# Linear attention and a feed-forward block in one kernel: products of four tiles at a time, loads of the attention units issued by ScalarE, two more denominators computed early

## The chip, the cores and the metric

The kernel runs on one NeuronCore of a Trainium2 chip, with TensorE (PE), VectorE (DVE), ScalarE (ACT), GpSimd (POOL) and SyncE (SP) as its engines. The metric is the device time of one execution in microseconds (us), as the median of several runs; lower is better. One of the executions was taken with a hardware profile, from which all views in this text come.

## The reference

A layer norm, multi-head linear attention with a learned feature map (two softmaxes over 32 values for each head, of a projection and of its negative), a residual; then a layer norm, a ReLU feed-forward block and a residual. There are 2048 tokens of width 1024, 32 heads of 32, and a hidden width of 3584, all in float32.

```python
qkv = layernorm(x) @ wqkv                    # (2048, 3 * 1024), 32 heads of 32
pq, pk = q @ w_phi[h], k @ w_phi[h]          # for each head
phi_q = concat(softmax(pq), softmax(-pq))    # 64 features a head; phi_k alike
kv = phi_k^T v ; z = sum over tokens of phi_k
o = (phi_q @ kv) / (phi_q @ z + 1e-6)
h = x + o @ wo
out = h + relu(layernorm(h) @ w1) @ w2
```

## The kernel before

**Products.** Every large product is made of three: TensorE multiplies a high and a low part of each operand (high x high, high x low, low x high; lines 181 to 183), 128x128 stationary and 128x512 moving. The parts of a weight tile come from `Units.advance`: ScalarE copies the loaded tile to the high part (line 124), and POOL or DVE subtracts to get the low part (line 128). Which of the two does it stands in `odd`. Tiles of w1 and w2 are also needed as sums and differences (the feed-forward block is multiplied by a seven-product scheme): `t_load` loads a set, `t_sum` makes four sums on POOL (line 378), `t_store` writes them to DRAM, from where they are loaded like weights later. There are 56 such sets.

**Order.** The work on TensorE is a list of items. An item is one 128-token tile against one group of weights: 8 steps, each of three multiplications (4 steps in the feed-forward part). Items 0 to 31 make keys and values of the first eight token tiles, in four slabs of 256 columns (eight items each); 32 to 47 the queries of these tiles; 48 to 79 keys and values of the last eight tiles; 80 to 95 their queries; 96 to 127 the output projection; then come the two products of the feed-forward block. Everything else is placed by hand at a step: `when(step, f, ...)` issues f behind step `step % 8` of item `step // 8`. What is issued goes to the engines' queues in that order, and each engine works through its own queue in order. SP issues nearly all DMAs, in order as well, and stands when one waits for a buffer.

**Keys and values.** Behind an item, `kv_first` (DVE) starts the softmax, `kv_exp` (ScalarE) and `kv_second` (DVE) finish it and leave `kphi` (line 472; four buffers), `kv_z` (POOL, line 480) adds it up, and `kv_third` (line 491) multiplies it with the values: 16 small multiplications a tile, 128x32 stationary. They are issued for three, three and two tiles of a slab together, at one place.

**Folds.** The projections' weights are multiplied with w_phi first, on TensorE: `fold_part(p)` (64 small multiplications, line 297; 32x32), `fold_turn` (DVE), `fold_store` to DRAM, and `fold_ready`, behind which the weights may be loaded. p = 0 to 3 are the four slabs, 4 to 7 the queries.

**Attention.** A unit u (32 of them) is four token tiles by 256 columns of features. `at_load` loads the exponentials of the queries (written to `ed` earlier), `at_sums` multiplies them with z on POOL (line 616, tile `ez`, one buffer), `at_reduce` sums on DVE (line 622), `at_den` (POOL, lines 631 and 635) and `at_inverse` (DVE) make the denominator, `at_scale` (POOL, lines 648 and 653) scales, `at_turn` (DVE, line 659) transposes 32x32 blocks, and `at_num` (TensorE, line 673) multiplies two units with kv; ScalarE copies the four results out, and `at_low` (DVE, line 690) makes the low parts. For units 0 to 5 (`EARLY`) load, sums, denominator and inverse are made once beside keys and values (`early_load` and so on), and the scale goes into a small tile; these units load again later and are only scaled. In each unit's list of steps, the denominators lie ahead of the unit's turn, and `at_num` follows some 30 steps behind the unit's start. Layer norm statistics of the second block (`ln_power` on POOL, `ln_pair`) lie between them.

**Opening.** Before item 0 and inside it, the first slab's weights are made: for each k of 8, `first_high` (ScalarE) copies a part of a PSUM tile, and `first_low` (DVE, line 415) subtracts from the same PSUM tile; two k share one.

Of the kernel before, what the change touches and what calls it, by code (L numbers as in the profile page):

```python
# [67 lines left out]
class Units:  # L68
# [35 lines left out]
    def advance(self, n):  # L104
# [7 lines left out]
        while self.done < self.loaded:  # L112
# [5 lines left out]
            if self.first[key] > n + SOON and n < max(self.asked[key] + LAG, self.latest + pace):  # L118
# [6 lines left out]
            odd = key[0] == "a" or key[0] in ("kv", "w1", "wo") and self.done % 2 or \  # L125
                key[:2] == ("q", 0) and key[-1] in (2, 5)
            eng = nc.vector if odd else nc.gpsimd
# [12 lines left out]
def kernel(  # L140
# [220 lines left out]
    def t_load(w, p, j, place):  # L361
        cols = slice(256 * j, 256 * (j + 1))
        if place is lnp:
            b = lnp.tile([P, D], F32, name="xin").rearrange("p (a f) -> p a f", a=4)
        else:
            b = place.tile([P, 4, 256], F32, name="b", bufs=2)
        src = (w1 if w == 1 else w2)[2 * p:2 * p + 2, :, :, cols]
        sp.dma_start(b, src.rearrange("a b p f -> p (a b) f"))
        for r in range(2):
            for c in range(2):  # L370
                tsum[j, r, c] = b[:, 2 * c + r if w == 1 else 2 * r + c, :]
        tsum[j] = b
# [210 lines left out]
    def at_load(u):  # L583

        e = lnp.tile([P, D], F32, name="xin") if u in (4, 5, 10, 11) else ap_.tile([P, D], F32, name="qe", bufs=4)
        e_q[u] = e = e.rearrange("p (h s f) -> p h s f", s=2, f=DH)
        sp.dma_start(e.rearrange("p (i c) s f -> p i (c s f)", i=4), ed[u // 8][:, u % 8])

    EARLY = 6

# [20 lines left out]
    def at_sums(u):  # L613
        b, q, r = UNITS[u]
        ez = ap_.tile([P, D], F32, name="ez", bufs=1).rearrange("p (i n) -> p i n", i=4)
        pool.tensor_tensor(out=ez, in0=e_q[u].rearrange("p (i h) s f -> p i (h s f)", i=4),  # L616
                           in1=zb[:, q, None, 256 * r:256 * (r + 1)].to_broadcast([P, 4, 256]), op=ALU.mult)
        ez_of[u] = ez

    def at_reduce(u):  # L620
        tz_of[u] = tz = ap_.tile([P, 32], F32, name="qtz", bufs=2)
        v.tensor_reduce(out=tz, in_=ez_of.pop(u).rearrange("p i (h f) -> p (i h) f", f=DH), op=ALU.add, axis=AX.X)

# [16 lines left out]
    def at_scale(u):  # L640
        if u < EARLY:
            e = e_q.pop(u).rearrange("p (i c) s f -> p i (c s) f", i=4)
# [331 lines left out]
    for i, j in enumerate((2, 3, 0, 1)):  # L974
# [3 lines left out]
        when(40, fold_ready, 0, j // 2)  # L978
    for p, n in zip(range(1, 8), (3, 8, 12, 16, 20, 24, 28)):
        do(n, 6 if p > 1 else 7, fold_part, p)  # L980
        if p > 1:
            when(8 * n + 10, fold_turn, p, (0, 1))
        for j in range(2):
            lag = 8 * n + 6 + 2 * j + (3 if p == 1 else 0)
            when(lag + (6 if p == 1 else 14), fold_store, p, j)
            when(lag + (13 if p == 1 else 24), fold_ready, p, j)
        do(max(n - 2, 1), 0, wt_load, p, sp)


    for (hf, s, t), n in kv_n.items():  # L990
        when(8 * n + 11, kv_exp, (hf, s, t))
        when(8 * n + 13, kv_second, (hf, s, t))
        when(8 * n + 18, kv_z, (hf, s, t))
        when(8 * (n + (2, 1, 0, 2, 1, 0, 1, 0)[t % HT]) + 22, kv_third, (hf, s, t))
        if hf == 1 and t == NT - 1:
# [67 lines left out]
    for u in range(32):  # L1063
        start = 8 * (a0 + u) if u >= 8 else 8 * (last_kv + 4) + 19 * u // 2
        slack = 6 if u < 5 else 0
        if u % 2:
            places = (-8 if u < 12 else -1, 6, 10, 13, 16, 19, 25)
            when(start + 30 + slack, at_num, u - 1)
            when(start + 32 + slack, at_low, u - 1)
        elif u < 16:  # L1070
            places = (-8 if u < 12 else -1, 6, 10, 13, 16, 19, 25)
        else:
            places = (6, 12, 16, 19, 21, 23, 29)
        for step, f in zip(places, (at_load, at_sums, at_reduce, at_den, at_inverse, at_scale, at_turn)):
            if u >= EARLY or f in (at_load, at_scale, at_turn):
                when(max(start + step, 8 * (last_kv + 4)), f, u)
        if u < EARLY:
            start = 8 * (kv_n[1, u // 2, NT - 1] + 3) + 4 + 18 * (u % 2)
            for step, f in ((0, early_load), (9, early_sums), (14, early_reduce), (16, at_den), (18, at_inverse),
# [50 lines left out]
    sets = [(w, p, j) for w in (1, 2) for p in range(NP) for j in range(2)]  # L1130
    places = [24 + 10 * n for n in range(22)] + [264, 274, 284, 294, 364, 374]
    slabs = [8 * kv_n[1, q, HT] for q in range(4)]
    places += sorted([slab + step for slab in slabs for step in (10, 24, 38)] + [slabs[1] + 2, slabs[2] + 2])
    places += [up0 + 440 + 25 * n for n in range(14)]
    for n, (step, (w, p, j)) in enumerate(zip(places, sets, strict=True)):
        far = n < 22
        when(step, t_load, w, p, j, lnp if step > up0 else fp if far and n % 4 > 1 else tsp)
        for k in range(4):
            when(step + (12 if far else 7) + k, t_sum, j, k)
        when(step + (19 if far else 13), t_store, w, p, j)  # L1140

# [72 lines left out]
    for k in range(2):  # L1214
        value_low(k, pool)
        first_high(k)
        first_low(k)
    first_fold(2)
# [3 lines left out]
    for k in range(2, 4):  # L1222
        first_high(k)
        first_low(k)
    ln_stats(("x", 1))
# [82 lines left out]
```

## Time and profile before

| | |
|---|---|
| time before, median of 3 runs | 1890.67 us (1890.42 to 1891.12) |
| the profiled execution | 1889.38 us, of which the span of instructions 1887.6 |
| busy: PE, DVE, ACT, POOL | 1876.9, 1070.4, 743.5, 983.7 us |
| granted TensorE clock | 1.000 |
| mean DMA rate | 229 GB/s |

In the views, a line of a timeline is start, length, engine, line of the code, operation, output <- inputs, shapes, and in brackets how long the engine stood before it and what ended that. "x" is a count. PEld is TensorE's weight load, which runs beside its multiplications. An engine that ends in q is the queue that issues.

### The profile page before, as it was taken

Reading aid. Unit: us, or ns where it says so; the run is one execution under the profiler, and the core shown is the slowest. Engines: PE = TensorE matmul, PEld = TensorE weight load, DVE = VectorE, ACT = ScalarE, POOL = GpSimd, SP = SyncE. Lnnn points to the kernel's source line nnn. Section 1 sums busy time; section 2 is a strip of 40 time slices with the busy share of each in tenths; the row PEclk is TensorE's granted clock in tenths of the full one; section 3 lists DMA queues with packets and bytes.
Section 4 is the critical chain, followed back from the end, with each engine's and each line's share of the span. In section 5 each row is a group of like instructions: output and inputs, shape, how many; then the busy total and the mean of one; then the engine's idle time right before and its main releaser. Section 6 shows DMA issues by size and latency. Waiting matters only on the chain.

```text
span 1887.6 us, 31801 instructions
## 1 busy us (share of the span) xinstructions
PE 1876.9 (99%) x11630; PEld 1538.0 (81%) x11630; DVE 1070.4 (57%) x1688; ACT 743.5 (39%) x1264; POOL 983.7 (52%) x934
## 2 busy tenths in 40 slices
PE   9999999999999999999999999999999999999999
PEld 7777888888888787888888888888888888888887
DVE  7888688676689667455444573445443433343333
ACT  5322244222233122354554554444344444444442
POOL 3888633677746888323333234544454444444443
PEclk9999999999999999999999999999999999999999
DMA  6799685454454666886777996787777677777775
GB/s 226 255 302 327 232 257 179 151 151 147 149 188 160 203 225 217 270 266 201 272 232 237 302 298 234 250 286 242 274 259 216 199 234 237 239 215 216 217 214 179
DMA packets 292749, 432.17 MB, mean 229 GB/s; under 512 B 24176, under 2 KB 150128, under 8 KB 292592
## 3 DMA queue, kind: packets, MB, share of 16 engines
q1 hardware_dynamic: 275424, 413.33, 68.3%
q10 hardware_dynamic: 17168, 16.81, 2.5%
q8 instruction: 91, 1.49, 0.3%
q14 instruction: 66, 0.54, 0.1%
HBM read 292.68 MB, written 137.36 MB: 228 GB/s over the span
## 4 chain that ended last, share of the span: by engine, by line
PE 92%; POOL 5%; DVE 2%; issue 1%; ACT 0%; DMA 0%; SPq 0%; POOLq 0%; DVEq 0%
PE mm L181 24%; PE mm L182 23%; PE mm L183 23%; PE ac L183 4%; PE ac L181 4%; PE ac L182 4%; PE tp L182 2%; PE tp L183 2%; PE tp L181 2%; POOL ez L616 1%; PE tp L250 1%; POOL qe L653 1%; PE ac L491 1%; PE tp L673 1%; POOL w L128 1%
## 5 line engine op out<-in xcount | busy, mean ns | idle before, releaser
L128 POOL TENSOR_TENSOR w<-raw,w 128x512 fp32r<-128x512 f32 x355 | 481.7, 1361 | 584.1 <-ACT w L124 571.4
L124 ACT ACTIVATE w<-raw 128x512 fp32r<-128x512 f32 x686 | 411.5, 629 | 488.4 <-PE mm L183 224.1
L128 DVE TENSOR_TENSOR w<-raw,w 128x512 fp32r<-128x512 f32 x331 | 281.3, 851 | 508.3 <-ACT w L124 505.2
L181 PE MATMUL mm<-w,xT 128*128 128x512 f32 x752 | 300.9, 400 | 0.0
L182 PE MATMUL mm<-w,xT 128*128 128x512 f32 x752 | 293.5, 390 | 0.6 <-POOL w L128 0.6
L183 PE MATMUL mm<-w,xT 128*128 128x512 f32 x752 | 293.1, 390 | 0.0
L181 PE MATMUL mm<-hT,w 128*128 128x512 f32 x672 | 262.6, 391 | 0.0
L183 PE MATMUL mm<-hT,w 128*128 128x512 f32 x672 | 261.6, 389 | 0.0
L182 PE MATMUL mm<-hT,w 128*128 128x512 f32 x672 | 261.5, 389 | 0.0
L378 POOL TENSOR_TENSOR b<-b 128x256 f32<-128x256 f32 x168 | 134.3, 800 | 87.7 <-DMA b<-in_w_dram 79.8
L181 PEld LDWEIGHTS mm<-w,xT 128*128 128x128 f32 x752 | 141.2, 188 | 33.3 <-issue 3.4
L183 PEld LDWEIGHTS mm<-w,xT 128*128 128x128 f32 x752 | 141.2, 188 | 30.2
L182 PEld LDWEIGHTS mm<-w,xT 128*128 128x128 f32 x752 | 141.3, 188 | 29.3 <-POOL w L128 1.1
L181 PE MATMUL mm<-w 128*128 128x512 f32 x392 | 152.5, 389 | 0.0
L182 PE MATMUL mm<-w 128*128 128x512 f32 x392 | 152.5, 389 | 0.0
L183 PE MATMUL mm<-w 128*128 128x512 f32 x392 | 152.5, 389 | 0.0
L183 PEld LDWEIGHTS mm<-hT,w 128*128 128x128 f32 x672 | 126.2, 188 | 26.4
L182 PEld LDWEIGHTS mm<-hT,w 128*128 128x128 f32 x672 | 126.2, 188 | 25.8
L181 PEld LDWEIGHTS mm<-hT,w 128*128 128x128 f32 x672 | 126.2, 188 | 25.6
L378 POOL TENSOR_TENSOR xin<-xin 128x256 f32<-128x256 f32 x56 | 48.9, 874 | 96.7 <-DMA xin<-in_w_dram 89.3
L480 POOL TENSOR_TENSOR zacc<-zacc,kphi 128x512 f32<-128x512 f32 x60 | 82.9, 1381 | 13.4 <-DVE kphi L472 13.4
L183 PEld LDWEIGHTS mm<-w 128*128 128x128 f32 x392 | 73.6, 188 | 15.2
(175 smaller groups left out, 3204.8 us busy)
## 6 DMA issues: line engine op xcount, KB each, us to landing
raw<-t SPq DMA_DIRECT2D x224, 256.0 KB, 4.2
raw<-ad SPq DMA_DIRECT2D x196, 256.0 KB, 3.0
raw<-in_w_dram SPq DMA_DIRECT2D x168, 256.0 KB, 3.4
ad<-c SPq DMA_DIRECT2D x112, 256.0 KB, 4.9
b<-in_w_dram SPq DMA_DIRECT2D x42, 512.0 KB, 5.3
t<-b SPq DMA_DIRECT2D x42, 512.0 KB, 3.7
ad<-s SPq DMA_DIRECT2D x84, 256.0 KB, 4.8
ed<-qe ACTq DMA_DIRECT2D x32, 512.0 KB, 3.6
```

The lines of the kernel that those rows point to most:

```text
L124: nc.scalar.activation(w[:, 0, :], raw[1], AF.Copy)
L128: eng.tensor_tensor(out=w[:, 1, :], in0=raw[1], in1=w[:, 0, :].bitcast(F32), op=ALU.subtract)
L181: pe.matmul(ps, a_hi, b_hi, start=first, stop=False, skip_group_check=more)
L182: pe.matmul(ps, a_hi, b_lo, start=False, stop=False, skip_group_check=more)
L183: pe.matmul(ps, a_lo, b_hi, start=False, stop=last, skip_group_check=more)
L250: pe.transpose(pt[:, k, :], xn[:, (4 * j + k) * P:(4 * j + k + 1) * P], ident)
L378: pool.tensor_tensor(out=tsum[j, *out], in0=tsum[j, *a], in1=tsum[j, *b], op=ALU.subtract)
L480: pool.tensor_tensor(out=zacc[s], in0=zacc[s], in1=phi_of[key], op=ALU.add)
L491: pe.matmul(kv_ps[s][g][32 * i:32 * (i + 1), 0:64], vt[:, 32 * h:32 * (h + 1)], phi[:, 64 * h:64 * (h + 1)], start=first, stop=last)
L616: pool.tensor_tensor(out=ez, in0=e_q[u].rearrange("p (i h) s f -> p i (h s f)", i=4), in1=zb[:, q, None, 256 * r:256 * (r + 1)].to_broadca ...
L653: pool.tensor_tensor(out=e, in0=e, in1=sd[:, :, None].to_broadcast([P, 32, 32]), op=ALU.mult)
L673: pe.matmul(banks[g][32 * c:32 * (c + 1), r * P:(r + 1) * P], kvL[rows, 4 * q + 2 * sd + h // 4, 32 * (h % 4):32 * (h % 4 + 1)], phT[rows, ...
```

## The change

- `Units.advance`: of the queries' weights in the second half, first column group, the tiles k = 2 and 5 get their low part on DVE instead of POOL (as in the first half).
- `t_load` in the feed-forward part and all `at_load` are issued by ScalarE instead of SP.
- `EARLY` gains units 10 and 11; their early steps start at 635 and 642.
- `at_sums` and `at_reduce` work in two halves of 512, with two buffers of 512 instead of one of 1024.
- From unit 16 on, `at_turn` of an odd unit moves from step 25 to 23 of the unit, and `at_reduce` of an even one from 16 to 17.
- `kv_third`: four tiles together, at 8(n + 3 - t % 4) + 20, instead of three, three and two.
- `fold_part` for p = 2 to 7 moves from place 6 of items 8, 12, ..., 28 to place 4 of items 9, 13, ..., 29, with all that follows.
- The sets of sums move: six of them in each 64 steps at -9, 0, 9, 18, 27 and 36 instead of one every ten; one more at 314; in the feed-forward part the sums come 11 steps behind the load instead of 7, and the stores' distance becomes 17 (13 beside keys and values).
- Opening: `first_high` for both k of a pair, then `first_low` for both.

```diff
             odd = key[0] == "a" or key[0] in ("kv", "w1", "wo") and self.done % 2 or \
-                key[:2] == ("q", 0) and key[-1] in (2, 5)
+                key[0] == "q" and key[1:3] != (1, 1) and key[-1] in (2, 5)
...
-        sp.dma_start(b, src.rearrange("a b p f -> p (a b) f"))
+        (act if place is lnp else sp).dma_start(b, src.rearrange("a b p f -> p (a b) f"))
...
-        sp.dma_start(e.rearrange("p (i c) s f -> p i (c s f)", i=4), ed[u // 8][:, u % 8])
+        act.dma_start(e.rearrange("p (i c) s f -> p i (c s f)", i=4), ed[u // 8][:, u % 8])
-    EARLY = 6
+    EARLY = {0, 1, 2, 3, 4, 5, 10, 11}
...
     def at_sums(u):
         b, q, r = UNITS[u]
-        ez = ap_.tile([P, D], F32, name="ez", bufs=1).rearrange("p (i n) -> p i n", i=4)
-        pool.tensor_tensor(out=ez, in0=e_q[u].rearrange("p (i h) s f -> p i (h s f)", i=4),
-                           in1=zb[:, q, None, 256 * r:256 * (r + 1)].to_broadcast([P, 4, 256]), op=ALU.mult)
-        ez_of[u] = ez
+        e = e_q[u].rearrange("p (i h) s f -> p i (h s f)", i=4)
+        ez_of[u] = []
+        for i in range(0, 4, 2):
+            ez = ap_.tile([P, 512], F32, name="ez", bufs=2)
+            pool.tensor_tensor(out=ez.rearrange("p (i n) -> p i n", i=2), in0=e[:, i:i + 2],
+                               in1=zb[:, q, None, 256 * r:256 * (r + 1)].to_broadcast([P, 2, 256]), op=ALU.mult)
+            ez_of[u].append(ez)
...
-        v.tensor_reduce(out=tz, in_=ez_of.pop(u).rearrange("p i (h f) -> p (i h) f", f=DH), op=ALU.add, axis=AX.X)
+        for i, ez in enumerate(ez_of.pop(u)):
+            v.tensor_reduce(out=tz[:, 16 * i:16 * (i + 1)], in_=ez.rearrange("p (n f) -> p n f", f=DH), op=ALU.add,
+                            axis=AX.X)
...
-    for p, n in zip(range(1, 8), (3, 8, 12, 16, 20, 24, 28)):
-        do(n, 6 if p > 1 else 7, fold_part, p)
+    for p, n in zip(range(1, 8), (3, 9, 13, 17, 21, 25, 29)):
+        step = 8 * n + (4 if p > 1 else 7)
+        when(step, fold_part, p)
         if p > 1:
-            when(8 * n + 10, fold_turn, p, (0, 1))
+            when(step + 4, fold_turn, p, (0, 1))
...
-        when(8 * (n + (2, 1, 0, 2, 1, 0, 1, 0)[t % HT]) + 22, kv_third, (hf, s, t))
+        when(8 * (n + 3 - t % 4) + 20, kv_third, (hf, s, t))
...
-            places = (-8 if u < 12 else -1, 6, 10, 13, 16, 19, 25)
+            places = (-8 if u < 12 else -1, 6, 10, 13, 16, 19, 25 if u < 16 else 23)
...
-            places = (6, 12, 16, 19, 21, 23, 29)
+            places = (6, 12, 17, 19, 21, 23, 29)
...
-            start = 8 * (kv_n[1, u // 2, NT - 1] + 3) + 4 + 18 * (u % 2)
+            if u < 6:
+                start = 8 * (kv_n[1, u // 2, NT - 1] + 3) + 4 + 18 * (u % 2)
+            else:
+                start = 8 * (last_kv + 1) + {10: -5, 11: 2}[u]
...
-    places = [24 + 10 * n for n in range(22)] + [264, 274, 284, 294, 364, 374]
+    places = [64 * q + step for q in range(4) for step in (-9, 0, 9, 18, 27, 36) if 64 * q + step > 9]
+    far_sets = len(places)
+    places += [264, 274, 284, 294, 314, 364, 374]
...
-            when(step + (12 if far else 7) + k, t_sum, j, k)
-        when(step + (19 if far else 13), t_store, w, p, j)
+            when(step + (12 if far else 11 if step > up0 else 7) + k, t_sum, j, k)
+        when(step + (13 if not far and step < up0 else 17), t_store, w, p, j)
...
         first_high(k)
+    for k in range(2):
         first_low(k)
```

More of the change, by code (lines that the diff above doesn't have):

```diff
@@ L640, in at_scale @@
     def at_scale(u):
-        if u < EARLY:
+        if u in EARLY:
             e = e_q.pop(u).rearrange("p (i c) s f -> p i (c s) f", i=4)
@@ L978 @@
         when(40, fold_ready, 0, j // 2)
-    for p, n in zip(range(1, 8), (3, 8, 12, 16, 20, 24, 28)):
-        do(n, 6 if p > 1 else 7, fold_part, p)
+    for p, n in zip(range(1, 8), (3, 9, 13, 17, 21, 25, 29)):
+        step = 8 * n + (4 if p > 1 else 7)
+        when(step, fold_part, p)
         if p > 1:
-            when(8 * n + 10, fold_turn, p, (0, 1))
+            when(step + 4, fold_turn, p, (0, 1))
         for j in range(2):
-            lag = 8 * n + 6 + 2 * j + (3 if p == 1 else 0)
-            when(lag + (6 if p == 1 else 14), fold_store, p, j)
-            when(lag + (13 if p == 1 else 24), fold_ready, p, j)
+            when(step + 2 * j + (8 if p == 1 else 14), fold_store, p, j)
+            when(step + 2 * j + (15 if p == 1 else 24), fold_ready, p, j)
         do(max(n - 2, 1), 0, wt_load, p, sp)
@@ L1072 @@
         else:
-            places = (6, 12, 16, 19, 21, 23, 29)
+            places = (6, 12, 17, 19, 21, 23, 29)
         for step, f in zip(places, (at_load, at_sums, at_reduce, at_den, at_inverse, at_scale, at_turn)):
-            if u >= EARLY or f in (at_load, at_scale, at_turn):
+            if u not in EARLY or f in (at_load, at_scale, at_turn):
                 when(max(start + step, 8 * (last_kv + 4)), f, u)
-        if u < EARLY:
-            start = 8 * (kv_n[1, u // 2, NT - 1] + 3) + 4 + 18 * (u % 2)
+        if u in EARLY:
+            if u < 6:
+                start = 8 * (kv_n[1, u // 2, NT - 1] + 3) + 4 + 18 * (u % 2)
+            else:
+                start = 8 * (last_kv + 1) + {10: -5, 11: 2}[u]
             for step, f in ((0, early_load), (9, early_sums), (14, early_reduce), (16, at_den), (18, at_inverse),
@@ L1130 @@
     sets = [(w, p, j) for w in (1, 2) for p in range(NP) for j in range(2)]
-    places = [24 + 10 * n for n in range(22)] + [264, 274, 284, 294, 364, 374]
+    places = [64 * q + step for q in range(4) for step in (-9, 0, 9, 18, 27, 36) if 64 * q + step > 9]
+    far_sets = len(places)
+    places += [264, 274, 284, 294, 314, 364, 374]
     slabs = [8 * kv_n[1, q, HT] for q in range(4)]
-    places += sorted([slab + step for slab in slabs for step in (10, 24, 38)] + [slabs[1] + 2, slabs[2] + 2])
+    places += sorted([slab + step for slab in slabs for step in (10, 24, 38)] + [slab + 2 for slab in slabs[1:3]])
     places += [up0 + 440 + 25 * n for n in range(14)]
     for n, (step, (w, p, j)) in enumerate(zip(places, sets, strict=True)):
-        far = n < 22
+        far = n < far_sets
         when(step, t_load, w, p, j, lnp if step > up0 else fp if far and n % 4 > 1 else tsp)
         for k in range(4):
-            when(step + (12 if far else 7) + k, t_sum, j, k)
-        when(step + (19 if far else 13), t_store, w, p, j)
+            when(step + (12 if far else 11 if step > up0 else 7) + k, t_sum, j, k)
+        when(step + (13 if not far and step < up0 else 17), t_store, w, p, j)
     for b in range(2):
@@ L1223 @@
         first_high(k)
+    for k in range(2, 4):
         first_low(k)
```

## The prediction

> **What bounds the kernel now.** I read first how busy each engine is in stretches of 50 us, then TensorE's waits, then the timelines around them. Stretches (length, then busy time and instruction count of PE, PEld, DVE, ACT, POOL; clock; DMA share):
>
> ```profile
> core 0 of [0], span 1887.6 us
> ...
> 500.00:550.00 50.00, 50.00 (x294) 40.81 (x295) 37.46 (x60) 13.84 (x19) 21.97 (x18) 1.00 0.51 170
> 600.00:650.00 50.00, 47.63 (x566) 37.98 (x565) 37.69 (x55) 9.41 (x22) 45.32 (x42) 1.00 0.62 203
> 700.00:750.00 50.00, 48.72 (x654) 39.04 (x657) 33.86 (x49) 13.44 (x24) 41.50 (x47) 1.00 0.62 206
> 800.00:850.00 50.00, 50.00 (x222) 41.43 (x221) 28.22 (x32) 28.09 (x42) 12.88 (x9) 1.00 0.85 270
> ```
>
> TensorE is the bound: without a pause from 500 and from 800 us, at a granted clock of 1.00, and in the plain stretch one multiplication takes 50/222 = 0.225 us. No other engine's time counts unless TensorE pauses for it. TensorE's own waits say where it does (total, times, longest; the two left-out ones lie in the first 8 us, ahead of anything the change touches):
>
> ```profile
> PE tp L673 <- issue: 2.5, 2, 2.2
> ...
> PE tp L250 <- DVE oT L690: 1.0, 1, 1.0
> PE mm L182 <- POOL w L128: 0.6, 1, 0.6
> ```
>
> So only two things can give time: 4.1 us of pauses, and multiplications that cost more than their share because TensorE changes from one shape to another.
>
> **Four tiles at a time.** kv_third multiplies with 128x32 operands between 128x128 ones. I cut out stretches from the start of the last 128x128 multiplication before such a visit to the start of the second one after it (the first one after starts late as well); less two ordinary steps (0.45 us), the rest is the visit's price. In order: a visit of two tiles, of three tiles, a fold_part alone, a fold_part followed at once by three tiles:
>
> ```profile
> 79.98:81.22 1.24, 1.24 (x36) 1.00 0.96 285
> 115.88:117.35 1.47, 1.47 (x52) 1.00 1.09 385
> 122.40:124.47 2.07, 2.07 (x67) 1.00 1.10 317
> 97.10:99.99 2.89, 2.89 (x115) 1.00 1.02 292
> ```
>
> Two tiles cost 1.24 - 0.45 = 0.79 us, three 1.02: a tile costs 0.23 and the visit itself 0.79 - 2 x 0.23 = 0.33 us. Now each slab of eight tiles is visited three times (3 + 3 + 2); afterwards twice (4 + 4). With eight slabs (four in each half) eight visits go: 8 x 0.33 = **2.65 us**. A visit of four is not in this trace; between a price per visit that stays (0.33) and one that grows in step (0.11 for the fourth tile, 16 x 0.11 = 1.8 lost) I take the first, since from two to three tiles it did not grow.
>
> **The folds move beside the sums.** fold_part alone costs 1.62, with three tiles 2.44: 1.62 + 1.02 - 2.44 = 0.20 saved where they are neighbours. The step of kv_third is now 8n+22 (place 6 of an item) and becomes place 4 of items 5, 9, 13, 17, 21, 25, 29, 33; fold_part for p = 2 to 7 moves from place 6 of items 8, 12, 16, 20, 24, 28 to place 4 of items 9, 13, 17, 21, 25, 29. Now three of six meet a kv visit (items 12, 20, 28), then all six: 3 x 0.20 = **0.6 us**. The rule in the Trainium skill, TensorEngine Tiling (Array Packing), Key Properties, is that changing the tiling mode drains TensorE; a fold beside a kv visit then needs three changes where two visits needed four, so as an estimate half of 0.33, 0.17 us, would be saved each time, and 0.5 in all where the rows give 0.6. The folds' stores and their release move along with them (fold_store still 14 steps behind); the weights of slab 2 are then asked for at steps 100 and 102 instead of 94 and 96 and needed from 128, so six steps of a lead of 34 go: cost nothing, the cover is those 28 steps (18 us).
>
> **The sums of w1 and w2 (t_load, t_sum, t_store).** Now they come every 10 steps, in the way of the weight splits ahead of a new slab. POOL and TensorE where the third wait ends:
>
> ```profile
> 69.62 1.18 POOL L378 TENSOR_TENSOR b<-b 128x256 f32<-128x256 f32 x1
> 70.76 1.72 POOL L128 TENSOR_TENSOR w<-raw,w 128x512 fp32r<-128x512 f32 x1
> ```
> ```profile
> 72.54 0.50 PE mm L182
> ```
>
> POOL does splits and sums in turn and is behind by four sums of about 1.2 us; the split that ends at 72.48 is what TensorE starts on at 72.54. Afterwards sets start at steps 18, 27, 36, 55, 64, ..., so t_sum lies at 48 to 51 and then at 67 to 70, and none between 52 and 66, where these splits are (54 to 60). This wait goes: 0.64 as idle time, 1.03 - 0.23 = 0.80 as the delay of the start (each wait costs 0.16 more than its idle time). What is late next is the slab's last split, on DVE (done at 71.35), which TensorE wants one step of three multiplications later: without the wait at 71.74 + 0.68 = 72.4, and 0.7 sooner where the visits cost less. So bounds 0 and -0.64, and I take **0.6**, at the full end because 4 x 1.2 us of POOL's work leave. The earlier first set (18 for 24) puts 0.5 MB into the opening's DMA traffic, and t_store of the second set stands ahead of raw loads on SP: bounds 0 and +0.8 (another wait of the size seen); I take 0.1 lost, since POOL has the time back.
>
> **Attention: denominators of units 10 and 11 early, loads by ScalarE, halves, turns first.** POOL from 597 to 633 (count, busy, mean ns):
>
> ```profile
> L616 POOL TENSOR_TENSOR ez<-xin,zb 128x1024 f32<-128x1024 f32 x2 | 4.8, 2388 | 0.0
> ...
> L631 POOL TENSOR_TENSOR qtz<-qtz,smq 128x32 f32<-128x32 f32 x5 | 3.2, 633 | 0.0
> L648 POOL TENSOR_TENSOR qsd<-smq,qden 128x32 f32<-128x32 f32 x5 | 1.8, 350 | 0.0
> L635 POOL TENSOR_TENSOR qden<-qtz 128x16 f32<-128x16 f32 x5 | 1.4, 281 | 0.4
> ```
>
> and the end of the longest wait, on SP, POOL, DVE and TensorE:
>
> ```profile
> 605.79 7.06 SPq L345 DMA_DIRECT2D raw<-in_wo_dram  x2
> ```
> ```profile
> 617.52 2.39 POOL L616 TENSOR_TENSOR ez<-qe,zb 128x1024 f32<-128x1024 f32 x1 [1.88 <-DMA qe<-ed]
> ...
> 621.45 1.92 POOL L653 TENSOR_TENSOR xin<-xin,qsd 128x1024 f32<-128x1024 f32 x1
> ```
> ```profile
> 624.52 1.19 DVE L659 STREAM_TRANSPOSE xin<-xin 128x1024 f32<-128x1024 f32 x1
> ```
> ```profile
> 625.81 0.34 PE L673 MATMUL tp<-xin,kvL 32*32 32x128 f32 x8 [2.23 <-issue]
> ```
>
> That last row is at_num of units 10 and 11; it waits for unit 11's turn on DVE, that for its scaling on POOL (621.45), and POOL is simply behind. Units 10 and 11 cost POOL 2 x (2.39 + 0.63 + 0.28 + 0.35) = 7.3 us here besides the scaling; this goes to steps 644 to 662, about 505 to 520 us, where POOL is busy 22 of 50 us and DVE 37. There it is covered by that idle time; without it the queries' splits and kv_z would be late. Two splits of ("q", 1, 0), k = 2 and 5, go from POOL to DVE in the same place. The 1.88 us for a load that SP issued after standing 7.06 us on a raw load go too, since ScalarE issues it. With 9 us off POOL ahead of a wait of 2.2, scaling ends near 614 and the turn near 616, ahead of 622.5. This wait is gone: **2.2**.
>
> The other wait of that line (0.3) and the 1.0 on oT come from DVE, which stands in order behind a reduce that POOL has not fed:
>
> ```profile
> 707.66 1.22 DVE L622 TENSOR_REDUCE qtz<-ez 128x32 f32<-128x1024 f32 x1 [2.03 <-POOL ez L616]
> ...
> 708.95 0.69 DVE L690 TENSOR_TENSOR oT<-tp,oT 128x256 fp32r<-128x256 f32 x2
> ```
> ```profile
> 709.37 0.66 PE L250 MATMUL tp<-ident,xin 128*128 128x128 f32 x4 [0.97 <-DVE oT L690]
> ```
> ```profile
> L616 POOL TENSOR_TENSOR ez<-qe,zb 128x1024 f32<-128x1024 f32 x16 | 38.2, 2388 | 9.2 <-DVE qtz L622 9.2
> ```
>
> The last row (POOL, 646 to 765 us) is the single ez buffer: POOL stands 9.2 us over 16 units until DVE has reduced the unit before. With two halves in two buffers most of that goes, and a reduce ends behind the second half alone (0.6 us sooner). The turn of an odd unit comes at step 23 ahead of the next unit's reduce. But two ln_power and both sums stay between 700 and 708 on POOL, and a load now comes behind at_num's four copies on ScalarE. Bounds for both waits: 0 and -1.3; I take **1.0**. The halves' cost, 24 more POOL instructions, is hidden by the 9.2 us. ScalarE gets 32 loads of ed and 14 t_loads that were SP's; where one waits for its buffer, the weight copies (L124) behind it wait too. The buffer is freed by an at_num that TensorE has passed by then, so I cost this at nothing; the cover is the ten steps that a copy is ahead of its use.
>
> **Opening copies in pairs.**
>
> ```profile
> 10.51 0.39 ACT L411 ACTIVATE w<-ac 128x256 fp32r<-128x256 f32 x1 [0.49 <-DVE w L415]
> ```
>
> ScalarE's second copy waits for DVE's subtraction on the same PSUM tile; in pairs that wait goes, but the first subtraction then starts behind two copies. TensorE needs both. Bounds +0.3 and -0.5; I take 0.1 gained. t_load by ScalarE and t_sum four steps later in the feed-forward part: TensorE shows no wait there, cost nothing; cover is DMA time ahead of POOL's sums, and if it were gone POOL's w1 splits would be late.
>
> **Sum.** 2.65 + 0.6 + 0.6 - 0.1 + 2.2 + 1.0 + 0.1 = 7.05, and 0.16 more for each of the four waits that go (0.6): 7.65. The profiled execution took 1889.38 us (span 1887.6 and 1.8 around it) and becomes 1881.7; it lies 1.3 under the median of the runs, 1890.67, which becomes **1883.0**.
>
> **Rivals.** *A new wait for the fourth tile (slower).* kv_third now takes the last of four tiles two steps earlier. DVE's phi of a slab's last tile, and TensorE at the new place of that visit; and the same for the first group of all:
>
> ```profile
> 411.30 1.40 DVE L472 TENSOR_TENSOR kphi<-ke,ksm 128x512 f32<-128x512 f32 x1
> ```
> ```profile
> 414.78 0.39 PE L181 MATMUL mm<-w,xT 128*128 128x512 f32 x1
> ```
> ```profile
> 49.22 0.69 DVE L472 TENSOR_TENSOR kphi<-ke,ksm 128x512 f32<-128x512 f32 x1
> ```
> ```profile
> 52.36 0.48 PE L181 MATMUL mm<-w,xT 128*128 128x512 f32 x1
> ```
>
> There are 414.78 - 412.70 = 2.1 us left, and in the opening 52.36 - 49.91 = 2.45 less the 1.0 of a visit that TensorE no longer makes before it: 1.4. For slower by 0.2%, 7.65 + 3.8 = 11.5 us must be lost over the eight last visits of the slabs, 1.4 each: DVE would have to be 3.5 us later in every one. Nothing adds that much to DVE there: 1895 us, chance 0.03. *The attention part stays late.* Loads of units 16 and up are issued at the step of an at_num, now behind its copies; if POOL gets them later than it gains by halves, the waits come back elsewhere. Then 3.8 of the gain fail: 1886.8, chance 0.14. The Trainium skill, DMA: Bandwidth & Descriptors, Issuing engines are not separate DMA queues, speaks for it: another issuing engine saves only the time to initiate a DMA; the 7.06 us above, which are waiting in order, speak against. *The first stage pays back.* The sums clumped into six of 64 steps make another split or load late by what the old one cost: 0.6 not gained, 0.8 lost, 1884.4, chance 0.15. *The change does not do what it says* would be visits that stay apart from the folds; the steps above exclude it.
>
> **How the numbers follow.** My case has 0.68 and its own range is 1881.3 (every bound at its good end) to 1884.0; the rivals reach 1884.4, 1886.8 and 1895. Leaving out the slower one and a little at each end, I give 1881.0 to 1887.2. A measurement tells about 0.2% (3.8 us) from no change, so faster means under 1886.9: my case, the first stage and a good half of the attention case, 0.86; the rest of it 0.11; slower 0.03.
>
> **What would show it.** L491 in 16 visits of 64 instead of 24; no wait of TensorE on L128 near 70 us; none on L673 near 620; DVE's reduce in 128x512 pieces and POOL's idle time before the ez sums well under 9.2 us; the ed loads on ACTq. The prediction is wrong if a visit of four costs over 1.25 us, if TensorE waits for kphi, or if POOL is behind at 700 us as now.

## The result, and the profile after

| | median, us | range, us | before beside it, us | ratio and 95% interval |
|---|---|---|---|---|
| new kernel | 1880.9 | 1879.8 to 1881.7 | 1890.5 | 0.9949 (0.9936 to 0.9961) |
| a second time | 1881.7 | 1880.6 to 1884.0 | 1890.9 | 0.9954 (0.9941 to 0.9968) |
| a third time | 1881.3 | 1880.8 to 1882.6 | 1890.6 | 0.9950 (0.9936 to 0.9963) |

Faster, by 9.1 us if all runs of the new kernel (median 1881.3) and of before (1890.5) are put together; the forecast was 7.65, and 1883.0. The first median lies 0.1 under the range's low end of 1881.0; the other two lie inside it. Line numbers of the new kernel are some higher than before's: at_num's L673 is now L678, ez's L616 is L619, oT's L690 is L695.

TensorE's waits in the new kernel, first profile (total, times, longest). The 1.6 us is the start, as before:

```profile
PE tp L1193 <- POOL ones L1189: 1.6, 1, 1.6
PE tp L1212 <- ACT xn L237: 1.2, 1, 1.2
PE tp L250 <- ACT xn L243: 0.4, 1, 0.4
PE mm L541 <- DVE w L415: 0.2, 1, 0.2
```

L673's 2.5 us, L250's 1.0 on oT and L182's 0.6 on GpSimd's w are no longer there. New is L250's 0.4 on xn: tile 6 of the stream is turned at 50.5 us and ScalarE's normalised tile comes that late now. The stretches (PE's busy time is the second number of the row):

```profile
600.00:650.00 50.00, 50.00 (x698) 40.48 (x697) 37.06 (x62) 10.52 (x25) 41.99 (x45) 1.00 0.67 228
700.00:750.00 50.00, 50.00 (x646) 40.74 (x623) 35.25 (x63) 12.03 (x26) 45.13 (x55) 1.00 0.69 225
```

Both stretches that had 2.4 and 1.3 us of pause have none. The two kinds of visit that are left, cut as the prediction cut them: a visit of four tiles alone, and a fold with four:

```profile
223.91:225.60 1.69, 1.69 (x68) 1.24 (x67) 0.32 (x2) 1.19 (x2) 0.25 (x1) 1.00 1.02 340
77.27:80.38 3.11, 3.11 (x132) 2.04 (x130) 1.31 (x5) 0.63 (x1) 2.88 (x5) 1.00 0.88 260
```

Less two steps of 0.23 that is 1.24 and 2.66 us. GpSimd before its ez (the same 16 units as in the prediction's last row on it, now in halves):

```profile
L619 POOL TENSOR_TENSOR ez<-qe,zb 128x512 f32<-128x512 f32 x32 | 40.9, 1304 | 5.6 <-DMA qe<-ed 5.2 <-DVE qtz L626 0.4
```

The wait for VectorE on the single buffer, 9.2 us, has become 0.4; what remains, 5.2, is for the loads of e.

### The profile page after: what moved, and what is told of

Same layout as the page of the kernel before. It is cut to its first block, busy times and chain, and to the rows that moved or that the text cites. A ratio compares the mean times of both kernels' runs of the same rounds, so it can differ in the third digit from the quotient of the medians.

```text
span 1879.7 us, 31869 instructions
## 1 busy us (share of the span) xinstructions
PE 1872.6 (100%) x11630; PEld 1540.3 (82%) x11630; DVE 1063.6 (57%) x1714; ACT 741.0 (39%) x1264; POOL 976.9 (52%) x956
## 4 chain that ended last, share of the span: by engine, by line
PE 98%; DVE 1%; ACT 0%; POOL 0%; DMA 0%; issue 0%; SPq 0%; DVEq 0%; POOLq 0%
PE mm L181 25%; PE mm L182 25%; PE mm L183 25%; PE ac L181 4%; PE ac L182 4%; PE ac L183 4%; PE tp L182 2%; PE tp L181 2%; PE tp L183 2%; PE tp L250 1%; PE tp L678 1%; PE ac L491 1%; PE ac L678 1%; PE tp L297 0%; DVE st L220 0%; PE tp L758 0%
## 5 line engine op out<-in xcount | busy, mean ns | idle before, releaser
L128 POOL TENSOR_TENSOR w<-raw,w 128x512 fp32r<-128x512 f32 x353 | 474.6, 1347 | 671.5 <-ACT w L124 638.0
L128 DVE TENSOR_TENSOR w<-raw,w 128x512 fp32r<-128x512 f32 x333 | 275.0, 827 | 512.9 <-ACT w L124 507.3
L182 PE MATMUL mm<-w,xT 128*128 128x512 f32 x752 | 293.0, 390 | 0.0
L182 PE MATMUL mm<-hT,w 128*128 128x512 f32 x672 | 261.5, 389 | 0.0
L378 POOL TENSOR_TENSOR b<-b 128x256 f32<-128x256 f32 x168 | 129.0, 769 | 85.2 <-DMA b<-in_w_dram 75.4
L182 PEld LDWEIGHTS mm<-w,xT 128*128 128x128 f32 x752 | 141.3, 188 | 28.5 <-issue 1.0
L182 PE MATMUL mm<-w 128*128 128x512 f32 x392 | 152.5, 389 | 0.0
L182 PEld LDWEIGHTS mm<-hT,w 128*128 128x128 f32 x672 | 126.2, 188 | 25.7
L181 PEld LDWEIGHTS mm<-w 128*128 128x128 f32 x392 | 73.6, 188 | 15.3
L182 PEld LDWEIGHTS mm<-w 128*128 128x128 f32 x392 | 73.6, 188 | 15.3
```

The lines of the kernel that those rows point to most:

```text
L128: eng.tensor_tensor(out=w[:, 1, :], in0=raw[1], in1=w[:, 0, :].bitcast(F32), op=ALU.subtract)
L181: pe.matmul(ps, a_hi, b_hi, start=first, stop=False, skip_group_check=more)
L182: pe.matmul(ps, a_hi, b_lo, start=False, stop=False, skip_group_check=more)
L378: pool.tensor_tensor(out=tsum[j, *out], in0=tsum[j, *a], in1=tsum[j, *b], op=ALU.subtract)
```

## The experiments

The medians of before that stand beside them were 1890.9 in the first four, 1891.0, 1889.7, 1890.4 and 1890.6 in the next groups.

**The parts alone.** The new kernel (second row of the table above):

> The whole change once more, beside the three runs that follow on the same chip. Theory A (the step that was too small is the attention term: nearly all of what I set against the earlier reads and the loads by ScalarE was short pauses that the view of waits does not list): 9.6 us below before (0.9949), and the three parts below make it up: 3.3 + 4.8 + 1.0. Rival B (the opening differs by luck of its DMAs, and the measured 9.6 contains 1 to 2 us of it): 7.9 to 9.0, as the spans of the two profiles differ by 7.9.

Measured: 1881.7, 9.1 below before, between the numbers of the two theories. The parts that follow do not make it up as theory A has it.

The visits and folds alone:

```
+ when(8 * (n + 3 - t % 4) + 20, kv_third, ...)          # four tiles
+ for p, n in zip(range(1, 8), (3, 9, 13, 17, 21, 25, 29)): step = 8 * n + (4 if p > 1 else 7)
```

> Before, with kv_third called for four tiles at a time and the folds ahead of the sums, nothing else. The prediction's terms: 2.65 + 0.6 + 0.16 for a wait gone = 3.3 less. Theory A: 2.6 to 3.4 less, the visits themselves 1.23 us (four tiles) and 2.65 us (fold and four). Rival C (the kv part is where the prediction was too small): 5 or more less.

Measured: 1890.0, ratio 0.9999 (0.9990 to 1.0008). Nothing that can be told from before, which neither theory had. Yet the visits do save time: from the start of item 48 to the start of item 80 the trace has 1.15 us less than before, as much as in the new kernel. Three items later, when the last of these visits are made, the new kernel has saved 1.78 us and this one 0.49: in between it waits 0.71 us on GpSimd's w (at 506.84), and the multiplication behind such a wait starts late too. TensorE's waits say where the rest went:

```profile
PE mm L182 <- POOL w L128: 2.6, 3, 1.2
PE tp L673 <- issue: 2.0, 2, 1.7
...
PE tp L250 <- DVE oT L690: 1.6, 1, 1.6
...
PE tp L673 <- POOL sc L230: 0.9, 1, 0.9
```

With the 0.4 on xn, and without the start, these are 7.5 us of waits, where before had 4.1: TensorE comes earlier, GpSimd does not. The wait on w near 73 us grows from 0.6 to 1.2 and two of 0.7 are new. And a wait costs more than its length. TensorE's granted clock (third number from the end) in this kernel around its wait of 1.7 us, a microsecond to a row:

```profile
624.00:625.00 1.00, 0.42 (x31) 0.15 (x17) 0.56 (x3) 0.00 (x0) 0.92 (x3) 1.00 1.11 195
625.00:626.00 1.00, 0.00 (x0) 0.00 (x0) 1.00 (x1) 0.00 (x0) 1.00 (x1) 1.00 0.94 336
626.00:627.00 1.00, 0.85 (x47) 0.76 (x57) 0.05 (x2) 0.00 (x0) 1.00 (x2) 0.53 1.07 227
627.00:628.00 1.00, 1.00 (x32) 0.62 (x25) 1.00 (x1) 0.49 (x2) 1.00 (x1) 0.50 0.96 242
628.00:629.00 1.00, 1.00 (x3) 0.76 (x3) 1.00 (x3) 0.72 (x3) 0.92 (x2) 0.50 0.86 334
629.00:630.00 1.00, 1.00 (x5) 0.78 (x4) 1.00 (x3) 0.00 (x0) 1.00 (x1) 0.76 0.75 291
630.00:631.00 1.00, 1.00 (x6) 0.84 (x5) 0.80 (x3) 0.00 (x0) 1.00 (x1) 1.00 0.16 64
```

Behind the wait the clock is at half for 3.4 us (called a fall from here on), so 1.7 us are lost besides the wait. In the profile of before, behind its longer wait (2.23 us, to 625.81), it is not:

```profile
626.00:627.00 1.00, 1.00 (x65) 0.74 (x44) 0.34 (x1) 0.30 (x2) 1.00 (x2) 1.00 0.95 277
627.00:628.00 1.00, 1.00 (x5) 0.83 (x5) 1.00 (x2) 0.92 (x4) 1.00 (x2) 1.00 0.89 287
```

The attention part alone (denominators of units 10 and 11 early, halves, ScalarE's loads, turns, splits):

```
+ EARLY = {0, 1, 2, 3, 4, 5, 10, 11}
+ act.dma_start(e..., ed[u // 8][:, u % 8])
+ for i in range(0, 4, 2): ez = ap_.tile([P, 512], F32, name="ez", bufs=2) ...
+ 25 if u < 16 else 23 (turn of odd units);  places = (6, 12, 17, 19, 21, 23, 29) (even)
```

> Before, with the attention part alone: denominators of units 10 and 11 beside the queries, ez in halves, loads by ScalarE, the turn and the split changed as in the new kernel. The prediction's terms: 2.2 + 1.0 + two restarts of 0.16 = 3.5 less. Theory A: 4.8 less (4.2 to 5.4), all visits of at_num at 2.03 us where before has seven longer ones. Rival C: 3.5 or less, as predicted.

Measured: 1886.0, 4.9 below before, 0.9972 (0.9963 to 0.9981), as theory A has it. In its trace the attention (items 80 to 127) took 4.1 less; left is a wait of 0.5 on oT.

The sums' places, their late loads by ScalarE and the pairs of copies alone:

```
+ places = [64 * q + step for q in range(4) for step in (-9, 0, 9, 18, 27, 36) if 64 * q + step > 9]
+ (act if place is lnp else sp).dma_start(b, ...);  first_low behind both first_high
```

> Before, with only the sums' new places, their far loads by ScalarE and the opening copies in pairs. The prediction's terms: 0.5 + 0.1 + 0.16 = 0.8 less. Theory A: 0.6 to 1.2 less, the wait on POOL near 72.5 us gone. Rival B (the opening is where before and after differ by more than the visits): 1.5 to 2.5 less, or more than 0.5 the other way, since the start is in this run as in the new kernel.

Measured: 1890.1, 0.8 less by the medians and 0.9996 (0.9987 to 1.0005). The wait near 72.5 is gone, items 8 to 31 take 0.74 less, and in the profiled run the wait on L673 grew from 2.2 to 3.0 in exchange. So the three parts alone bring 0.8, 4.9 and 0.8, together 6.5; all at once bring 9.1. (Of these three, only the attention's gain is clear of the noise.)

**Two parts of three.** Without the sums and the pairs, and without the visits and folds:

> Before, with kv_third by four tiles, the folds ahead of it and the whole attention part; the sums' places and the opening as before. It asks where the 3.3 us go that kv_third's visits save and that the run with the visits alone kept 0.8 of at most. Theory D (what a visit saves is lost again at the next wait on an engine that TensorE does not set: GpSimd's split of w near 72 us while the sums lie there, the late e in the attention): the attention gives the 4.9 of its own run and no longer takes 2.2 (items 48 to 79) back, items 8 to 31 still lose theirs: 7.0 to 7.5 us below before, the waits on POOL w L128 at 2 us or more. Rival A (only the attention takes it back): 8.2 below, the wait on POOL w L128 at 0.6.

> The new kernel with kv_third in twos and threes and the folds where they were: the attention part, the sums' places and the opening. Theory D (the sums' new places give little by themselves, and give the visits' gain room): 4.9 + 0.8 = 5.7 us below before, so that the visits are worth 3.3 in the new kernel, as predicted. Rival E (the attention part is worth more when TensorE does not arrive early at it): 6.5 or more below.

Measured: 1883.5, 7.5 below before, 0.9961 (0.9948 to 0.9973), with theory D; and 1885.1, 5.8 below, 0.9971 (0.9960 to 0.9982), as D also says. The first one's wait on GpSimd:

```profile
PE mm L182 <- POOL w L128: 1.9, 2, 1.2
```

So with the attention in order the visits bring 2.6 of their 3.3 or so (7.5 less the 4.9 of the attention alone), and with the sums out of the way all of it: by the traces of items 1 to 95 the new kernel takes 3.5 us less than the kernel without the visits. The third pair, the new kernel with the sums at their old places:

```
- places = [64 * q + step ...]
+ places = [24 + 10 * n for n in range(22)] + ...
```

> The new kernel with the sums at their old places (opening copies in pairs kept). The prediction set 0.6 against the sums, as one wait on POOL w L128 of 0.6 us. Theory D (the wait of 0.6 grows when TensorE comes 2.8 us earlier, as it did to 1.9 in two waits in the run without sums and opening): 1.5 to 2.5 us above the new kernel, waits on POOL w L128 at 1.9 us. Rival A (the term is the one wait of before): 0.6 above.

Measured: 1884.3, 5.4 below before's 1889.7, 0.9971 (0.9960 to 0.9981); 3.0 above the new kernel by the medians, and 2.6 in items 8 to 31 of the trace, where the wait on POOL w L128 is 1.9 us again (two waits). Theory D, a little more than it had. By the traces the sums' new places are worth 0.74 us by themselves and 2.6 when TensorE comes early.

**Which edit of the attention.** The new kernel with one edit taken back each time, and two edits put alone into before:

```
noload:    + sp.dma_start(e..., ed[u // 8][:, u % 8])
noearly:   + EARLY = 6   (and the splits of w as before)
nohalves:  + ez = ap_.tile([P, D], F32, name="ez", bufs=1)   (one multiplication, one reduce)
noturn:    + turn of odd units at 25, reduce of even ones at 16
loadonly:  before, + act.dma_start(e..., ed[u // 8][:, u % 8])
earlyonly: before, + EARLY = {0, ..., 5, 10, 11} (and the splits)
```

> The new kernel with at_load's DMAs issued by SP again. Prediction's step: the wait of 2.23 us on L673 goes because ScalarE's queue takes the loads of e past the weights that wait in SP's. Theory F (the queue is what does it): 2 to 4 us above the new kernel, ez's GpSimd idle again for 5 us or more near 615 us. Rival G (units 10 and 11 made early and ez in halves do it): within 0.5 us of the new kernel.

> The new kernel without the early denominators of units 10 and 11 and without the two more splits of w by VectorE beside them. Theory G (moving these sums out of the attention is what frees GpSimd there): 2 to 4 us above the new kernel, waits on L673 near 620 us again. Rival F (ScalarE's loads do it alone): within 0.5 us of the new kernel, ez's idle as small as there.

> Before with one word changed: at_load's DMAs issued by ScalarE in place of SP. Theory F (the prediction's: e waits in SP's queue behind weights, and the longest wait, 2.23 us on L673 near 620 us, goes with the queue): 2.2 to 3.5 us below before, and ez's GpSimd idle near there gone. Rival G (the new kernel with SP's loads was as fast as with ScalarE's, 1881.17 against 1881.74, so the queue does nothing): within 0.5 us of before, the wait on L673 still near 2 us. Of before's medians on this chip 1890.9: F 1887.5 to 1888.7, G 1890.4 to 1891.4.

> Before with only the denominators of units 10 and 11 done early and the two further splits of w per query item by VectorE. Theory G (two units less on GpSimd in the stage where it is late do it; the new kernel without this is 2.4 to 3 us slower): 2.5 to 4.5 us below before, no wait on L673 over 0.5 us between 610 and 640 us. Rival F: within 1 us of before. If both this run and the one with ScalarE's loads gain, each alone suffices and the two terms were counted once; if neither does, the halves or the turn matter.

| | median, us | ratio to before, 95% interval |
|---|---|---|
| noload | 1881.2 | 0.9949 (0.9937 to 0.9961) |
| noearly | 1884.1 | 0.9962 (0.9950 to 0.9975) |
| loadonly | 1892.2 | 1.0010 (1.0001 to 1.0019) |
| earlyonly | 1886.4 | 0.9984 (0.9975 to 0.9993) |

The early units do it, as theory G has it, and the loads by ScalarE do nothing: noload is as fast as the new kernel, earlyonly 3.3 us below before, noearly 2.8 above the new kernel (its wait near 620 us is only 0.6). For loadonly theory G had no change, and it came out 2.6 us slower than before. In the kernel with the loads alone unit 12's ez no longer stands 1.88 us on its load, and TensorE's wait at 625.67 is 0.35 us where it was 2.23, as the prediction said. But the same lateness comes out at 696:

```profile
696.03 0.34 PE L673 MATMUL tp<-qe,kvL 32*32 32x128 f32 x8 [2.31 <-issue]
```

GpSimd had as much to do as before, and behind this wait the clock fell to 0.50 again. With the early units alone the waits are

```profile
PE tp L250 <- DVE oT L690: 0.8, 1, 0.8
PE mm L182 <- POOL w L128: 0.7, 1, 0.7
PE tp L673 <- issue: 0.3, 1, 0.3
```

The Trainium skill, DMA: Bandwidth & Descriptors, Issuing engines are not separate DMA queues, says that issuing from more engines saves only the time of initiating. Here that was so: 0 us (noload against the new kernel).

> The new kernel with at_sums in one multiplication of 128x1024 into one ez and at_reduce in one, as before. Prediction's step: the halves let VectorE start on the first while GpSimd does the second (GpSimd idle before ez 9.2 us in before). Theory L (the halves bring what the early units don't: 1.6 of the attention's 4.9): 1 to 2 us above the new kernel, waits on L678 near 700 us. Rival M (the turn does): within 0.5 us.

> The new kernel with at_turn of the odd units from 17 on at step 25 in place of 23 and at_reduce of the even ones at 16 in place of 17. Theory M (VectorE's order is what left the short waits of 0.3 on L673 and 1.0 on oT): 1 to 2 us above the new kernel, a wait on L678 near 715 us of 0.3 or more. Theory L: within 0.5 us.

Measured: 1885.4, 0.9974 (0.9964 to 0.9984), and 1882.9, 0.9960 (0.9947 to 0.9972): 4.1 and 1.6 above the new kernel's 1881.3. Without the halves it is theory L, and more than it had: GpSimd stands again before its ez, VectorE's oT is late, and seven of eight runs show a fallen clock. Without the turn the time is what theory M had, but the wait that it named, near 715 us, is not there; the profile has 1.6 on oT, which differs by run in the new kernel too, so the turn's part is at the edge of what these runs tell. In nohalves:

```profile
L616 POOL TENSOR_TENSOR ez<-qe,zb 128x1024 f32<-128x1024 f32 x16 | 38.2, 2389 | 13.5 <-DVE qtz L622 10.3 <-DMA qe<-ed 3.2
```
```profile
PE tp L250 <- DVE oT L690: 3.0, 1, 3.0
```
```profile
708.00:709.00 1.00, 1.00 (x5) 0.90 (x4) 0.00 (x0) 0.47 (x1) 0.92 (x3) 0.50 0.42 164
```

**The wait on oT that is left.** It was 0.0, 1.0 and 0.8 us in three profiles of the new kernel, 2.9 in noload's. VectorE in the second, in order: two reductions that wait for GpSimd, then at_low's oT:

```profile
700.51 0.69 DVE L626 TENSOR_REDUCE qtz<-ez 128x16 f32<-128x512 f32 x1 [0.57 <-POOL ez L619]
701.11 0.24 DVE L643 RECIPROCAL qden<-qden 128x16 f32<-128x16 f32 x1
701.27 0.69 DVE L695 TENSOR_TENSOR oT<-tp,oT 128x256 fp32r<-128x256 f32 x2
```

and GpSimd ahead of that: it stands 2.46 us for unit 24's e, and does two ln_power between units 24 and 25 (from 695.43 to 697.94):

```profile
692.80 2.54 POOL L619 TENSOR_TENSOR ez<-qe,zb 128x512 f32<-128x512 f32 x2 [2.46 <-DMA qe<-ed]
695.43 0.22 POOL L229 TENSOR_SCALAR sc<-mv 128x1 f32<-128x1 f32 x1
...
697.94 2.53 POOL L619 TENSOR_TENSOR ez<-qe,zb 128x512 f32<-128x512 f32 x2
```

Two ways to take it, VectorE's order (late25) and GpSimd's (lnfirst):

```
late25:   + if u == 25: places = (-1, 6, 17, 18, 19, 20, 24)
lnfirst:  + places = (6, 13 if u == 24 else 12, 17, 19, 21, 23, 29)
```

> The new kernel with one line more: VectorE reduces unit 25's products (and GpSimd and VectorE its denominators) after at_low of unit 22 and not ahead of it. In the second profile of the new kernel VectorE's at_low stood behind two reductions that wait for ez of unit 25, whose e landed late, and TensorE waited 1.0 us on oT for the bank (2.9 in the run with SP's loads, 0.0 in the first profile, whose opening was 1.45 later). Theory H (the order on VectorE is the wait): no wait on oT, 0.4 to 1.0 us below the new kernel. Rival I (the reduction put behind comes late itself, and unit 24's or 25's multiplication waits instead): no gain, a wait on L678 near 710 us.

> The new kernel with at_sums of unit 24 one step later, so that GpSimd does the two ln_power of that step (2.5 us) while it would wait for e of unit 24, and not between the multiplications of units 24 and 25. Theory H2 (the wait on oT that is left, 0 to 2.9 us by run, is a chain: e of unit 24 lands late, GpSimd does ln_power behind it, unit 25's ez is late, VectorE's reductions hold at_low, TensorE waits on oT): the wait on oT at most 0.3, 0.5 to 1.2 us below the new kernel. Rival I2 (ScalarE's order, at_num behind ln_norm, or the loads hold it): no gain.

late25: 1881.6, no gain, as rival I has it, but not by its wait: TensorE waited 2.0 us on oT, because the inverse of unit 24 (one step that I had left ahead of at_low) waited 4.35 us on GpSimd and held it as the reductions had. lnfirst: no wait on oT at all,

```profile
693.81 0.27 POOL L231 TENSOR_SCALAR sc<-mv,sc 128x1 f32<-128x1 f32 x1
694.04 5.04 POOL L619 TENSOR_TENSOR ez<-qe,zb 128x512 f32<-128x512 f32 x4
```

the ln_power run while the load is under way and the four multiplications without a break. 1880.7, 0.9950 (0.9936 to 0.9963): the wait is shown gone, the time (0.6 under the new kernel) can't be told from it.

**A wait put back.** Three more multiplications for unit 13, the first half once more and the second twice, with the same values:

```
+ for _ in range((2 if i else 1) if u == 13 else 0): pool.tensor_tensor(out=ez..., in0=e[:, i:i + 2], ...)
```

> The new kernel with three of unit 13's multiplications into ez done twice or three times (the same values; 3 x 1.29 = 3.9 us more on GpSimd), so that at_num of units 12 and 13 waits some 2 to 3 us near 630 us, as before did near 624. Theory J (a wait costs its length, and in part of the runs TensorE's granted clock falls to 0.50 for 3.4 us behind it, worth 1.7 us): the runs at mean clock 1.000 are 2 to 3 us above the new kernel, a third or more of the runs show 0.999 or less and are 1.5 to 2 us above the others. Rival K (before's 0.999 comes from elsewhere in the program): all runs 2 to 3 us above, clocks 1.000 as in the new kernel.

Measured: 1883.0 and a wait, at another instruction than meant (the split of a weight that follows on GpSimd):

```profile
PE mm L182 <- POOL wf L128: 1.8, 1, 1.8
```

Four runs at clock 1.000 took 1882.0 to 1883.4, one at 0.999 took 1888.3. The four have a median of 1882.7, 1.4 above the new kernel, for a wait of 1.8; one run in five with a fallen clock is fewer than I expected, and its 5 us are more than one fall. This run alone does not decide for J; the clocks of the other kernels' runs are set out below.

**Both waits out.** lnfirst, and the turns of tile 6 a step later; beside it the new kernel again:

```
+ 6: (25, 33, 35, 37, 42, 45)
```

> The new kernel with at_sums of unit 24 a step later and the two turns of stream tile 6 a step later (42 and 45 in place of 41 and 44). Theory H2 (the late chain to oT is gone, and the turn of tile 6 a step later finds xn ready): waits of L250 on oT and on xn (L243, 0.4) gone, 0.8 to 1.5 us below the new kernel beside it. Rival I3 (item 6 then waits for xT): no gain in the opening items, 0.3 to 1.0 us below by the wait on oT alone.

> The new kernel a third time. Theory J: clocks 1.000 in all or all but one of its runs, median 1880.9 to 1881.8, 8.7 to 9.7 us below before's median and 7.7 to 8.3 below before's runs at clock 1.000, which is the prediction's sum of 7.65. Rival K (the clock has no part in the difference): the same distance to before's runs at 1.000 as to all of them, 9 us or more.

Measured: 1880.0 (1879.3 to 1880.3), 0.9941 (0.9929 to 0.9954), against 1881.3 of the new kernel beside it: theory H2, 1.3 us less, the fastest of all kernels here and the one that varies least. By the two traces 0.5 of it lies in items 1 to 7 and 1.0 in items 80 to 127. The new kernel's five runs beside it were all at clock 1.000, as theory J has it; they lie 9.3 us below the nine runs of before, and 8.5 below the only one of these at 1.000, which by itself can't decide between J and K. All waits of the fastest kernel:

```profile
PE tp L1212 <- ACT xn L237: 1.8, 1, 1.8
PE tp L1193 <- POOL ones L1189: 1.6, 1, 1.6
PE mm L541 <- DVE w L415: 0.2, 1, 0.2
```

## Why the prediction was right or wrong

**The step that failed is the last of the sum: "it lies 1.3 under the median of the runs, 1890.67, which becomes 1883.0".** I carried the 1.3 us over as if they would stay in the new kernel's median, and no bound allowed for less. (The good ends of the bounds add up to 8.5 us, which gives 1882.1 and not the 1881.3 that the prediction states.) Before's runs by their mean granted clock, beside those of other kernels:

| | runs | of them at 0.999 or less | longest wait past the start in the profile |
|---|---|---|---|
| before | 82 | 52 | 2.2 on L673 |
| rest | 11 | 7 | 3.0 on L673 |
| loadonly | 11 | 10 | 2.3 on L673 |
| nohalves | 8 | 7 | 3.0 on oT |
| kvfold | 11 | 5 | 1.7 on L673 |
| wait3 | 5 | 1 | 1.8 on wf |
| noload, late25, noturn | 15 | 0 | 2.9, 2.0, 1.6 on oT |
| norest, nokv, noearly, nosets | 25 | 4 | 1.2, 0.8, 0.7, 1.2 |
| earlyonly | 11 | 1 | 0.8 on oT |
| att | 10 | 2 | 0.6 on w |
| new kernel | 16 | 1 | 1.0 on oT (in one profile also 1.2 and 0.9 on ScalarE's c near 1100 us) |
| lnfirst and best | 10 | 0 | 0.4 on xn |

Before's median at 1.000 (30 runs) is 1889.2, at 0.999 (45 runs) 1890.8: 1.6 us apart, and 3.4 us at half clock are 1.7 us, or 0.0009 of the mean clock. Most runs of before lost that; the profiled one, at 1.000, did not. That it is lost behind the long wait, and not in the start, is seen from earlyonly and att: their start is before's to the letter, the long wait is gone, and with it nearly all the falls: 3 of 21 runs are left. (A fall can also stand in the start, as the profiles of kvfold and nosets show. The rows with oT say that length alone does not decide; oT's wait also differs by run.) So most of the 1.3 us was no constant between a profile and its median but a cost of the wait that the change removes. From the profiled time of 1889.38 the same sum gives 1881.7, which is inside the range and 0.4 above the median of the new kernel's runs; against before's runs at 1.000 the new kernel is 7.9 us faster, where the sum has 7.65.

That the sum is so near at equal clock is in part luck. From item 1 to item 127, where no profile of the two kernels has a fall, the three profiles of the new kernel took 9.3, 8.1 and 8.2 us less than before's; the sum without the opening has 7.55. So the terms were short as well, by 0.6 to 1.8 us: visits and folds by 0.2, the sums by 0.1 to 0.3, and the attention by the rest, most of all in the first profile, which has no wait on oT. Slow starts (1.5 us, see Opening) in two of the new kernel's profiles and two waits on ScalarE's c (2.1 us) in the third hide it. In how many of the other runs such things happened can't be told from their mean clocks, so how the difference of the medians divides between the clock and the terms stays open to about a microsecond.

The terms, in order:

- **Four tiles, 2.65, and folds, 0.6: right in size.** 1.24 and 2.66 us for the visits where 0.33 + 4 x 0.23 gives 1.25; a fold beside a visit of four saves 1.62 + 1.23 - 2.66 = 0.2. By the traces of items 1 to 95, new kernel against the one without: 3.5 where the two terms have 3.25. The rule of the Trainium skill, TensorEngine Tiling (Array Packing), Key Properties, that a change of mode drains TensorE gave an estimate of 0.17 for each fold, and the trace has 0.2. What the sum did not say is the condition: alone, 0.8 at most. "Only two things can give time" treats pauses and visits as independent, and they are not: what TensorE saves ahead of a wait, the wait takes.
- **Sums, 0.6 + 0.16 - 0.1: right alone (0.74), short in company (2.6 in items 8 to 31).** The wait of 0.64 near 72.5 would have become 1.2, and another of 0.7 would have come at 173, as in the run without these edits. These are the visits' saving, which the sum has under its own term, so the total is not short by it. (Of the four sums that the prediction counts at about 1.2 us, one took 0.74.)
- **Attention, 2.2 + 1.0 and the restarts of its three waits: mis-sized, 3.7 where the part alone brought 4.9.** In its trace it is 4.1, at clock 1.00, with 0.5 of oT's wait still there; the other 0.8 of the medians fit what the clock cost before. The cause was half wrong. "Go too, since ScalarE issues it": the loads by ScalarE brought nothing, and alone moved the wait from 625 to 696. The early units and the halves are what did it. The 1.0 on oT mostly stayed (1.0 and 0.8 in two of three profiles), because "two ln_power and both sums stay between 700 and 708", which the prediction saw and took to be bearable.
- **Restart, 0.16 for each wait:** too simple. It holds where the clock stays; where it falls a wait costs 1.7 more.
- **Opening, 0.1:** nothing measured. The first transposes to item 0 take 2.6 us in thirteen profiles and 4.1 to 4.3 in seven others, of kernels with either opening; in two of these seven (kvfold, nosets) the recorded clock is 0.50 there, and the first profile of the new kernel took 1.97 us for the eight transposes where before took 1.09:

```profile
7.78 1.97 PE L1212 MATMUL tp<-ident,xn 128*128 128x128 f32 x8 [1.17 <-ACT xn L237]
```
```profile
7.61 1.09 PE L1202 MATMUL tp<-ident,xn 128*128 128x128 f32 x8 [0.99 <-ACT xn L237]
```

  The recorded clock is 1.00 there, so in that profile only the durations show it. This lengthens the new kernel's first profile by 1.5 us and before's not at all, and is one reason why the two spans shown differ by 7.9 and the medians by 9 and more.
- **Rivals:** no wait for kphi anywhere, the fourth tile is ready, in 16 visits of 64 small multiplications; the attention did not stay late; the first stage paid back nothing but 0.6 us at tile 6's turn (50.5 us), which I had not seen and which goes when it turns a step later. In the prediction's chances the attention case (0.14) counts as faster with 0.03, which is a fifth of it and not the "good half" of the text.

Shown: the early units, the halves, the sums' places and the visits, each by its own run. Shown by the clocks of many runs and by four traces with a fall behind a wait (kvfold, rest, loadonly, nohalves), not by the run made for it: that the clock has a share. Open: what decides, run by run, whether a wait lowers the clock; late25's wait of 2.0 and noload's of 2.9 on oT did not in the executions profiled.

## What to carry to other kernels

Before a saving on the bounding engine is added up, ask for each wait behind it whether the engine waited for moves along; if it doesn't, the saving is only the sum over stretches between such waits, and the edits must be made together (0.8 + 4.9 + 0.8 alone, 9.1 at once). Where the profiled execution and the median differ, look at the granted clock of each before carrying the difference over: it may be the price of the very wait that is being removed. And a late engine is helped by taking work from it, not by handing it its input sooner.

## What the hardware showed that I had not expected

TensorE's granted clock fell to 0.50 for 3.4 us behind waits of 1.7 (kvfold), 2.3 (loadonly) and 3.0 us (rest, nohalves) in some executions, and stayed at 1.00 behind 2.2 (before), 2.0 (late25) and 2.9 us (noload) in others; at 0.50 a 128x512 step takes 427 ns where it takes 227. The Trainium skill, TensorE: Matmul & The Clock Gate, Part 1: The HAM clock gate, says that the clock halves after an idle window of about 3.4 us and that the window runs free of the program, so that it varies by run. The half and the 3.4 us agree with the rows above, and so does the variation; but the waits that were enough, 1.7 to 3.0 us, are shorter than that window, where small multiplications of 32x32 stood ahead of them (kvfold, loadonly, rest) and also where 128x512 ones did (nohalves).
